# A fused attention, routing and channel-mixing kernel: the distance tables on VectorE and GpSimd, and the early gather some turns later

## The chip, the cores and the metric

One core of a Trainium2 chip runs the whole program. The metric is the device time of one execution in microseconds (us), as the median of three. The engines are named as in the profile: PE (TensorE, with PEld for its weight loads), DVE (VectorE), ACT (ScalarE), POOL (GpSimd) and SP (SyncE, here the issuer of most DMA transfers).

## The reference

Three stages follow one another, for 2 sequences of 768 tokens.

```
attention: 8 heads of 64, keys 0..7 for everybody and the last 96 keys
    scores = q k^T / 8 - slope[h] * dist;  masked;  a = softmax;  out = a v
mixture of experts: logits = x w_gate (8 experts), gate = sigmoid(x w_local)
    e = argmax(logits) where gate < 0.5 (or first token), else the token before's e
    out = softmax(logits)[e] * relu(x w1[e]) w2[e]
mixer: u = x + real(fft over sequence and channels);  out = u + relu(norm(u) w_ch1) w_ch2
```

`dist` is the distance from query to key (96 for a far global key), and `slope[h]` is 2 to the power of -(h+1) for 8 heads. A bias table for each head is therefore one distance table times one number.

## The kernel before, in words

**Attention.** A tile is 128 queries. The queries are worked in 24 units, numbered 0 to 23: tile i (0 to 5), sequence b (0 or 1), head group g (4 heads). Unit n stands for (i, b, g) in that order. A tile sees its own keys (the right third of a table, columns 256 to 383) and those of the tile before (columns 0 to 255, the far part with the left neighbour and the own keys side by side). Tile 0 has only the near part, so units 0 to 3 read only that.

The loop over n issues parts of four units in a written order. In round n it issues: `out(n-2, 1)` (ACT, PSUM to SBUF copy of turned probabilities), `keep(n-3)` (DVE, L180, the product with v out of the PSUM tile `sm`), `scores(n)` (PE), `rowmin(n)` (DVE, L142: four operations that add a head's bias and find the minimum), `step(k)`, `transp(n-1, 0)` (PE), `expo(n)` (ACT, L151: four exponentials) with `den` (POOL, L152), `out(n-1, 0)` (ACT), `step(k+1)`, `transp(n-1, 1)`, `upright(n-3)` (PE, L185), `norm(n-3)` (DVE), `step(k+2)`, `values(n-2)` (PE, L175), `step(k+3)`. Each engine works through its own instructions in the order of issue.

**Background work.** Each `step` takes one step of every generator in a list; I call it a turn. There are four to a unit. The generators are `tables` (bias tables), `far`, `Route.run` for a finished tile, and `ring.take`, which splits a piece of expert weights into a rounded half `hi` (ACT cast, L1006) and a remainder `lo` (a subtraction, L1008), in four parts of 128x512 with a cast and a subtraction in alternating turns. Four pieces are taken, from the turns in `TAKES`: from the third turns of units 12, 16, 20 and 22 on.

**Routing.** `Route.run(i)` gets logits from a tile (`lg`), finds the expert by `max` and `max_index`, transposes two flags into `rp` on PE (L516, L517, into the same PSUM tile `sm` that `keep` reads), scans along the tokens, finds the place of each token, and writes the rows to `xs` (SP) and the places to `list` (POOL, an indirect DMA, L568). The operations on X stand on POOL, and on DVE for the last tile. The route of tile i begins when unit 4i+3 is done, three units after its scores, so that of tile 4 starts in unit 22 and its `rp` comes right after `values(21)`.

After tile 2 the route also reads the first 128 entries of the list of expert 0 (`ent0`, SP, L579), `EARLY_READ` turns after the list was written, and `EARLY_GATHER` turns later gathers those rows into `x0` (POOL, L582). `early` computes expert 0 for them; its PE transposes of `x0` (L840) stand ahead of `values(23)` in PE's order. After the last unit, the route of tile 5, its list, `entries`, and `gathers` for the other experts follow one another; PE's next stage begins with the transposes of gathered rows (L1103).

**Bias tables.** All are ACT operations before (L222): four near tables before the loop, one more near table in each of the first four turns, eight far tables from unit 1 on.

Of the kernel before, what the change touches and what calls it, by code (L numbers as in the profile page):

```python
# [17 lines left out]
AF = mybir.ActivationFunctionType  # L18
ALU = mybir.AluOpType
# [5 lines left out]
B, H, S, D = 2, 8, 768, 64  # L25
E, F = 8, 1024
DM = H * D
NT = S // P
# [24 lines left out]
def load_kq(nc, st, io, i, pairs=((0, B * H // 2),)):  # L53

    if i >= NT:
        return
    for h, n in pairs:
        nc.sync.dma_start(st.kq[i][:, :, h:h + n], io["kq"][i, :, :, h:h + n])


def fast_attention(tc, st, io, route):
    nc = tc.nc
    V, A, G, T = nc.vector, nc.scalar, nc.gpsimd, nc.tensor
    KS = 3
    HP = B * H // 2
    with ExitStack() as ctx:
# [12 lines left out]
        four, last = views(st.raws, PIECES), views(more, NT - PIECES)  # L79
# [8 lines left out]
        def load_v(i):  # L88
            nc.sync.dma_start(vs[:, i % KS], io["v"][i])
# [118 lines left out]
        bias = res.tile([P, H, 384], F32, name="bias")  # L208
# [3 lines left out]
        dist, gl = room[:, :384], room[:, 512:512 + P]  # L212

        def local(r, c):
            d = dist[:, c:c + P]
            V.tensor_scalar(d, r, nl, -BIG, op0=ALU.is_ge, op1=ALU.mult)
            V.scalar_tensor_tensor(d, r, -1.0, d, op0=ALU.mult, op1=ALU.min)
            return d

        def tables(lo, hi):  # L220
            for h in range(H):
                A.activation(bias[:, h, lo:hi], dist[:, lo:hi], AF.Copy, scale=8.0 * 2.0 ** -(h + 1))  # L222
                yield

        def far():
            d = local(prev, 0)
            V.tensor_tensor(d, d, gl, op=ALU.max)
            load_v(1)
            yield
            yield from tables(0, 256)  # L230
            load_kq(nc, st, io, 2)
            load_kq(nc, st, io, 3)

# [3 lines left out]
        V.tensor_scalar(gl, glob, ng, -BIG, op0=ALU.is_ge, op1=ALU.mult)  # L237
        V.tensor_scalar(gl, gl, neg_nl, None, op0=ALU.min)
        V.tensor_tensor(dist[:, 256:], d, gl, op=ALU.max)
        near = tables(256, 384)  # L240
        for _ in range(4):
            next(near)
        bg = Background()
        bg.add(near)
# [13 lines left out]
        def step(k):  # L258

            for at, g, lo, hi in TAKES:  # L260
                if k == at:
                    bg.add(st.ring.take("e", g, cols=512, follow=False, part=(lo / 4, hi / 4), eng=lambda: G))
            route.slot = k % 4
            bg.step()
            for _ in range(AHEAD.get(k, 0)):
                next(ahead, None)

        for n in range(N + 3):
            if ok(n):
                i, b, g = units[n]  # L270
# [8 lines left out]
            if n == 1:  # L279
                bg.add(far())  # L280
# [10 lines left out]
            if ok(n - 3) and not ok(n - 1):  # L291
                upright(n - 3)
                norm(n - 3)
            step(k)
            if n < len(BUSY):
                keep_busy(nc, st, ps_t.tile([P, 2, 2, P], F32, name="tp").rearrange("p a b n -> p (a b n)"), BUSY[n])
# [4 lines left out]
            if ok(n - 1):  # L301
                out(n - 1, 0)
            step(k + 1)
            if ok(n - 1):
                transp(n - 1, 1)
                if ok(n - 3):
                    upright(n - 3)
                    norm(n - 3)
            step(k + 2)
            if ok(n - 2):  # L310
                values(n - 2)
# [17 lines left out]
def general_attention(tc, st, io, route):  # L329
# [3 lines left out]
    with ExitStack() as ctx:  # L333
# [18 lines left out]
        for i in range(NT):  # L352
# [11 lines left out]
            for b in range(B):  # L364
                x = rt.tile([P, ROW], F32, name="xrow")
                xs.append(x)
                for h in range(H):
# [16 lines left out]
                    V.tensor_tensor(t, t, far, op=ALU.add)  # L384
                    V.tensor_reduce(out=m, in_=t, op=ALU.max, axis=AX.X)
                    V.tensor_scalar(m, m, -1.0, None, op0=ALU.mult)
                    A.activation(t, t, AF.Exp, bias=m)
                    V.tensor_reduce(out=m, in_=t, op=ALU.add, axis=AX.X)
                    V.tensor_scalar(m, m, 1e-9, None, op0=ALU.add)
# [40 lines left out]
class Route:  # L430
# [31 lines left out]
    def run(self, i, xs, parts=None):  # L462
        nc, st, sb = self.tc.nc, self.st, self.sb
        V, A, G, T = nc.vector, nc.scalar, nc.gpsimd, nc.tensor
# [8 lines left out]
        pp = sm[:, 0:B]  # L473
        other = sm[:16, 4:5]
        last, first = i == NT - 1, i == NT - 4
        X = V if last else G
        to = lambda s, n=1: self.at(None if last else s, n)
        from2, from1 = st.pairs[:16, 0:16], st.pairs[:16, 16:32]
        lg = sb.tile([P, B, NL], F32, name="lg")
        if parts is not None:  # L480
            V.tensor_reduce(out=lg.unsqueeze(3), in_=parts.rearrange("p b h e -> p b e h"), op=ALU.add, axis=AX.X)
        else:
# [22 lines left out]
        for b in range(B):  # L505
            V.max(m8[:, b], l8[:, b])
        X.tensor_scalar(gn, z.to_broadcast([P, B, E]), GATE, None, op0=ALU.is_ge)
        for b in range(B):
            V.max_index(ix[:, b], m8[:, b], l8[:, b])
        yield from to(1)  # L510
        V.tensor_copy(fr, ix[:, :, :1])
        X.tensor_tensor(pe, l8, m8[:, :, :1].to_broadcast([P, B, E]), op=ALU.subtract)
        V.scalar_tensor_tensor(gf, z.to_broadcast([P, B, E]), GATE, fr.to_broadcast([P, B, E]),
                               op0=ALU.is_lt, op1=ALU.mult)
# [7 lines left out]
        yield from to(1)  # L522
        V.tensor_reduce(out=su, in_=pe, op=ALU.add, axis=AX.X)
        if last:
# [3 lines left out]
        if last:  # L528
# [3 lines left out]
                             op0=ALU.mult, op1=ALU.add)  # L532
# [8 lines left out]
                             op0=ALU.mult, op1=ALU.add)  # L541
# [23 lines left out]
        for b in range(B):  # L565
# [3 lines left out]
                out=st.list, out_offset=bass.IndirectOffsetOnAxis(ap=pos[:, b:b + 1], axis=0),  # L569
# [3 lines left out]
        if first:  # L573

            V.tensor_scalar(su[:1, 0], less, 0.0, None, op0=ALU.max)
            V.tensor_tensor(cu[:1, P - 1:], cu[:1, P - 1:], su[:1, 0], op=ALU.add)
            for _ in range(EARLY_READ):
                yield
            nc.sync.dma_start(st.ent0, st.list[1:P + 1])  # L579
            for _ in range(EARLY_GATHER):  # L580
                yield
            G.indirect_dma_start(  # L582
                out=st.x0, out_offset=None, in_=st.xs[:(i + 1) * B * P], in_offset=bass.IndirectOffsetOnAxis(ap=st.ent0[:, 0:1], axis=0),
# [43 lines left out]
DC = 258  # L627
TABLES = 4 * E
EARLY = 4
EARLY_READ = 5  # L630
EARLY_GATHER = 5
LATE = 4
TAKES = ((-46, 0, 0, 4), (-30, 1, 0, 4), (-14, 2, 0, 4), (-6, 3, 0, 4))
SPLIT = 6
# [710 lines left out]
class Mixer:  # L1345
# [46 lines left out]
    def tables(self):  # L1392
        v = lambda t, o, a, n: t[:, o:o + a * n].rearrange("p (a n) -> p a n", a=a)
        ring = self.st.ring
        (ch, cl), (sh, sl) = ring.get("t", 0), ring.get("t", 1)
        self.c1, self.s1 = ([v(t, 0, 3, SC) for t in x] for x in ((ch, cl), (sh, sl)))
        self.odd = self.s1[0][:1, 0]
        self.c2, self.s2 = ([v(t, 3 * SC, 2, DC) for t in x] for x in ((ch, cl), (sh, sl)))
# [389 lines left out]
@with_exitstack  # L1788
def program(ctx, tc, io):
    nc = tc.nc  # L1790
    ctx.enter_context(tc.manual_schedule())
    st = setup(tc, ctx, io)
    load_kq(nc, st, io, 0, ((0, 2), (2, 2), (4, 4)))
    with tc.tile_pool(name="ps_busy", bufs=1, space=PSUM) as ps:
        keep_busy(nc, st, ps.tile([P, 512], F32, name="busy"), 12)
    fast = nc.values_load(st.fast[0:1, 0:1], min_val=0, max_val=1)
    with tc.If(fast > 0) as arm:
        fast_attention(tc, st, io, Route(tc, st, io))
    with arm.Else():
        general_attention(tc, st, io, Route(tc, st, io))  # L1800
    post(tc, ctx, st)
    moe = Moe(tc, st, io)
    mix = Mixer(tc, st, io, moe)
    with ExitStack() as c2:
        moe.open(c2)
        moe.run()
        moe.close_x.close()
        mix.begin(ctx, ExitStack())
        moe.finish()
    with ExitStack() as c2:  # L1810
        mix.open(c2)
        mix.run(c2)
# [11 lines left out]
```

## Time and profile before

| what | value |
|---|---|
| median of 3 runs | 656.48 us (655.08 to 660.21) |
| profiled execution, its own time | 658.99 us |
| its span, first to last instruction | 657.2 us |
| mean granted PE clock | 0.976 |
| PE, DVE, ACT, POOL busy | 95%, 59%, 42%, 16% of the span |

The attention stage takes about the first 115 us of the span and the experts follow. The PE share counts pipelined matmuls and says little of how full PE is. What matters here are the places in which PE waits, what ends those waits, and the clock after them.

### The profile page before, as it was taken

How to read it: one execution, taken by the hardware profiler on the slowest of the kernel's cores; microseconds unless marked ns; L12 is line 12 of the kernel's file. 1: busy time of each engine (PE TensorE's matmuls, PEld its weight loads, DVE VectorE, ACT ScalarE, POOL GpSimd, SP SyncE). 2: the span in 40 equal slices, each digit the busy share in tenths (PEclk: the TensorE clock that was granted, in tenths of full speed). 3: DMA queues.
4: the chain of work that ended last, by engine and by line, in shares of the span. 5: the costliest groups of instructions: out<-in, count | busy, mean ns of one | idle time of the engine just before them, and what ended most of it. 6: DMA issues, size and time to landing. Idle time of an engine off the chain costs nothing.

```text
span 657.2 us, 9964 instructions
## 1 busy us (share of the span) xinstructions
PE 623.8 (95%) x3621; PEld 511.4 (78%) x3622; DVE 387.4 (59%) x891; ACT 278.9 (42%) x562; POOL 102.1 (16%) x147
## 2 busy tenths in 40 slices
PE   7999986869999999999999899999999999999997
PEld 3787865558998998897867787877788888888885
DVE  4687784429967888853369977899441131254112
ACT  5789891117654756563434533441221221141110
POOL 1126636330431333220100000000000000000000
PEclk9999995969999999999999899999999999999999
DMA  8354463258899798873062143443010010100001
GB/s 298 142 179 155 134 91 115 45 209 276 296 369 325 239 320 316 301 285 143 21 243 93 65 135 122 163 157 129 0 65 0 1 65 1 65 0 1 0 1 64
DMA packets 25187, 92.45 MB, mean 141 GB/s; under 512 B 7644, under 2 KB 8796, under 8 KB 17184
## 3 DMA queue, kind: packets, MB, share of 16 engines
q1 hardware_dynamic: 19376, 77.41, 34.6%
q0 software_dynamic: 4736, 10.56, 4.4%
q10 hardware_dynamic: 1008, 3.65, 1.5%
q8 instruction: 35, 0.57, 0.4%
q14 instruction: 32, 0.26, 0.2%
HBM read 81.00 MB, written 14.84 MB: 146 GB/s over the span
## 4 chain that ended last, share of the span: by engine, by line
PE 43%; DVE 7%; ACT 2%; issue 1%; DVEq 0%; ACTq 0%
PE h L1636 17%; PE acc L1652 5%; PE acc L1650 5%; PE acc L1651 5%; DVE dec L1032 1%; DVE dec L1034 1%; PE acc L1471 1%; PE y L1141 1%; PE acc L1457 1%; PE more L1191 1%; PE f L1602 1%; PE more L1141 1%; PE h L1191 1%; DVE dec L1030 1%; DVE dec L1028 1%
## 5 line engine op out<-in xcount | busy, mean ns | idle before, releaser
L1641 DVE SCALAR_TENSOR_TENSOR hl<-h,hh 128x512 fp32r<-128x512 f32 x48 | 33.1, 689 | 118.4 <-ACT hh L1640 118.4
L1640 ACT ACTIVATE hh<-h 128x512 fp32r<-128x512 f32 x48 | 28.7, 597 | 153.4 <-PE h L1636 153.3
L1008 DVE TENSOR_TENSOR wide<-raws,wide 128x1024 fp32r<-128x1024 f32 (+1 forms) x38 | 45.0, 1200 | 24.4 <-ACT wide L1006 24.1
L151 ACT ACTIVATE t<-t,nm 128x256 f32<-128x256 f32 (+1 forms) x96 | 45.8, 478 | 7.5 <-DVE nm L142 7.5
L1006 ACT CAST wide<-raws 128x1024 fp32r<-128x1024 f32 (+2 forms) x46 | 43.3, 957 | 5.6 <-PE acc L1652 3.4
L1636 PE MATMUL h<-un0h,wide 128*128 128x512 f32 (+1 forms) x136 | 42.5, 378 | 0.0
L1651 PE MATMUL acc<-wide,hh 128*128 128x512 f32 x96 | 37.7, 393 | 0.0
L142 DVE CUSTOM_DVE_ANT_0 t<-sp,bias 128x256 f32<-128x256 f32 (+1 forms) x96 | 32.7, 396 | 8.4 <-PE sp L133 3.9
L1650 PE MATMUL acc<-wide,hh 128*128 128x512 f32 x96 | 37.7, 392 | 0.0
L1652 PE MATMUL acc<-wide,hl 128*128 128x512 f32 x96 | 37.5, 391 | 0.0
L1164 ACT ACTIVATE hh<-h 128x512 fp32r<-128x512 f32 x28 | 16.7, 598 | 30.1 <-PE h L1161 23.1
L1071 POOL DMA_INDIRECT xg<-xs,ent x23 | 26.9, 1167 | 14.3 <-issue 6.1
L1161 PE MATMUL h<-xh,wide 128*128 128x256 f32 x192 | 28.4, 284 | 0.5 <-DVE hl L1165 0.4
L1636 PEld LDWEIGHTS h<-un0h,wide 128*128 128x128 f32 x136 | 25.0, 188 | 4.7
L161 PE MATMUL tp<-consts,t 128*128 128x128 f32 x176 | 27.0, 292 | 0.4
L1161 PEld LDWEIGHTS h<-xh,wide 128*128 128x128 f32 x192 | 25.5, 192 | 1.3 <-DVE hl L1165 0.6
L161 PEld LDWEIGHTS tp<-consts,t 128*128 128x128 f32 x176 | 20.0, 146 | 8.3 <-ACT p L167 3.0
L175 PE MATMUL sm<-p,vs 128*64 128x128 f32 x352 | 26.3, 293 | 0.0
L1636 PE MATMUL h<-un0l,wide 128*128 128x512 f32 (+1 forms) x68 | 25.7, 378 | 0.0
L1165 DVE SCALAR_TENSOR_TENSOR hl<-h,hh 128x512 fp32r<-128x512 f32 x28 | 19.2, 686 | 10.6 <-ACT hh L1164 6.7
L167 ACT COPY p<-tp 128x512 f32<-128x512 f32 (+1 forms) x48 | 24.2, 534 | 0.0
L175 PEld LDWEIGHTS sm<-p,vs 128*64 128x64 f32 x352 | 20.2, 145 | 4.1 <-issue 3.8
(454 smaller groups left out, 1658.2 us busy)
## 6 DMA issues: line engine op xcount, KB each, us to landing
raws<-we SPq DMA_DIRECT2D x30, 1024.0 KB
raws<-wm SPq DMA_DIRECT2D x17, 1024.0 KB
raws<-wmf SPq DMA_DIRECT2D x7, 1024.0 KB
wmf<-dec POOLq DMA_DIRECT2D x8, 512.0 KB
xs<-xrow SPq DMA_DIRECT2D x12, 260.0 KB
vs<-v SPq DMA_DIRECT2D x6, 512.0 KB
raws<-kq SPq DMA_DIRECT2D x3, 1024.0 KB
u<-x SPq DMA_DIRECT2D x6, 512.0 KB
```

The source lines that it names most:

```text
L142: V.tensor_tensor_reduce(out=u.t[:, x, :u.W], in0=u.sp[:, j, k, :u.W], in1=bias[:, 4 * u.g + x, u.b0:u.b0 + u.W], scale=-0.125, scalar=3.0 ...
L151: A.activation(u.t[:, x, :u.W], u.t[:, x, :u.W], AF.Exp, bias=u.nm[:, x:x + 1], scale=-1.0, accum_out=u.den[:, x])
L161: T.transpose(u.tp[k][:, j, c], u.t[:, 2 * k + j, c * P:(c + 1) * P], st.ident)
L175: T.matmul(turned[j * D:j * D + D, k], vs[:, ti % KS, u.h + 2 * k + j], u.p[:, 2 * k + j, c], start=c == 0, stop=c == len(tiles) - 1)
L1006: (first or nc.scalar.copy)(hi[:, cs], raw[:, cs])
L1008: (eng() if callable(eng) else eng or nc.vector).tensor_tensor(lo[:, cs], raw[:, cs], hi[:, cs].bitcast(F32), op=ALU.subtract)
L1161: T.matmul(ps[:, u], w[:, f], x[:, k], start=n == 0, stop=n == 11)
L1636: nc.tensor.matmul(ps[:, c], a[:, k], x[:, k, c], start=n == 0, stop=n == 11)
L1641: nc.vector.scalar_tensor_tensor(hl, ps, 0.0, hh.bitcast(F32), op0=ALU.max, op1=ALU.subtract)
L1650: T.matmul(acc[c], hh[:, cs], h2, start=first, stop=False)
L1651: T.matmul(acc[c], hh[:, cs], l2, start=False, stop=False)
L1652: T.matmul(acc[c], hl[:, cs], h2, start=False, stop=last)
```

## The change

The far tables are DVE multiplications. The near tables are four on ACT and four on POOL, all issued before the loop. A piece's subtractions get their engine from a new expression. X is DVE for the tiles 4 and 5 (before, for 5 alone). The read of `ent0` waits for 10 turns and the gather for 7 more (before 5 and 5).

```diff
-        def tables(lo, hi):
+        def tables(lo, hi, by):
             for h in range(H):
-                A.activation(bias[:, h, lo:hi], dist[:, lo:hi], AF.Copy, scale=8.0 * 2.0 ** -(h + 1))
+                out, slope = bias[:, h, lo:hi], 8.0 * 2.0 ** -(h + 1)
+                if by[h] is A:
+                    A.activation(out, dist[:, lo:hi], AF.Copy, scale=slope)
+                else:
+                    by[h].tensor_scalar(out, dist[:, lo:hi], slope, None, op0=ALU.mult)
                 yield
...
-            yield from tables(0, 256)
+            yield from tables(0, 256, [V] * H)
...
-        near = tables(256, 384)
-        for _ in range(4):
+        near = tables(256, 384, [A] * 4 + [G] * 4)
+        for _ in range(H):
             next(near)
...
-                    bg.add(st.ring.take("e", g, cols=512, follow=False, part=(lo / 4, hi / 4), eng=lambda: G))
+                    bg.add(st.ring.take("e", g, cols=512, follow=False, part=(lo / 4, hi / 4), eng=lambda: G if at < TAKES[-1][0] else V))
...
-        X = V if last else G
+        X = G if i < NT - 2 else V
...
-EARLY_READ = 5
-EARLY_GATHER = 5
+EARLY_READ = 10
+EARLY_GATHER = 7
```

## Rows read from the trace of the kernel before

**Rows 1.** Timeline of PE, 95 to 113 us: start, duration, instruction, [idle before, releaser].

```profile
95.92 1.09 PE L175 MATMUL sm<-p,vs 128*64 128x128 f32 x16
103.51 0.27 PE L516 MATMUL sm<-identb,gn 128*16 128x128 bf16 x1 [6.50 <-POOL gn L507]
...
111.12 1.06 PE L840 MATMUL tp<-consts,x 128*128 128x128 f32 x4
```

**Rows 2.** Timeline of POOL in the same stretch.

```profile
94.70 1.13 POOL L582 DMA_INDIRECT x<-xs,ent  x1 [5.05 <-ACT wide L1006]
...
103.15 0.31 POOL L507 TENSOR_SCALAR gn<-lg 128x16 bf16<-128x16 f32 x1
```

**Rows 3.** Waits of the SP queue, 70 to 100 us: total, times, longest; then SP's timeline.

```profile
SPq L579 <- DMA list<-dest,pos: 6.4, 1, 6.4
89.27 0.33 SPq L579 DMA_DIRECT2D ent<-list  x1
```

**Rows 4.** Busy time by stretch: PE, PEld, DVE, ACT, POOL, granted clock, DMA.

```profile
97.00:103.00 6.00, 0.01 (x2) 0.00 (x0) 3.10 (x6) 1.74 (x5) 5.37 (x8) 0.70 0.31 118
103.00:108.00 5.00, 4.49 (x26) 3.99 (x28) 1.82 (x5) 2.05 (x5) 4.74 (x8) 0.50 0.01 0
```

**Rows 5.** Timeline of PE in the first 21 us.

```profile
13.43 1.24 PE L50 MATMUL tp<-busy 128*128 128x512 bf16 x4 [1.41 <-ACT p L167]
14.73 1.11 PE L161 MATMUL tp<-consts,t 128*128 128x128 f32 x4
15.78 1.12 PE L175 MATMUL sm<-p,vs 128*64 128x128 f32 x8
...
18.88 0.66 PE L161 MATMUL tp<-consts,t 128*128 128x128 f32 x4
...
19.97 0.66 PE L175 MATMUL sm<-p,vs 128*64 128x128 f32 x8
```

**Rows 6.** Timeline of ACT in the first 21 us, table rows.

```profile
8.34 1.11 ACT L222 ACTIVATE bias<-vs 128x128 f32<-128x128 f32 x5 [4.66 <-DVE vs L239]
...
10.89 0.69 ACT L222 ACTIVATE bias<-vs 128x128 f32<-128x128 f32 x3
```

**Rows 7.** Groups by line and form, all of the span: busy us, mean ns | idle before.

```profile
L1028 DVE TENSOR_SCALAR dec<-dec 128x1024 f32<-128x1024 f32 x18 | 12.4, 688 | 0.6 <-ACT dec L1019 0.6
L455 POOL COPY iw<-consts 128x512 f32<-128x512 f32 x1 | 0.9, 917 | 0.0
L152 POOL TENSOR_SCALAR den<-den 128x4 f32<-128x4 f32 x24 | 5.5, 228 | 47.7 <-ACT t L151 47.3
L1424 DVE TENSOR_TENSOR fs<-u 128x512 f32<-128x512 f32 x6 | 4.1, 677 | 1.7 <-DMA u<-x 1.7
L1008 POOL TENSOR_TENSOR sl0l<-raws,sl0h 128x512 fp32r<-128x512 f32 x4 | 5.1, 1276 | 0.7 <-ACT sl0h L1006 0.4 <-issue 0.2
```

**Rows 8.** Timeline of DVE, from the first attention units and the last ones.

```profile
16.97 0.42 DVE L180 COPY o<-sm 128x256 f32<-128x256 f32 x1 [3.34 <-PE sm L175]
...
95.70 3.27 DVE L511 CAST fr<-ix 128x2 f32<-128x2 uint32 x1
...
114.15 0.41 DVE L180 COPY o<-sm 128x256 f32<-128x256 f32 x1
```

**Rows 9.** Timeline of ACT, 53 to 60 us: one unit while a weight piece is taken.

```profile
55.22 0.51 ACT L151 ACTIVATE t<-t,nm 128x256 f32<-128x256 f32 x1
...
57.20 0.57 ACT L167 COPY p<-tp 128x512 f32<-128x512 f32 x1
57.66 0.62 ACT L1006 CAST sl0h<-raws 128x512 fp32r<-128x512 f32 x1
...
59.18 0.52 ACT L151 ACTIVATE t<-t,nm 128x256 f32<-128x256 f32 x1
```

**Rows 10.** Timeline of PE: the flags of the route of tile 2, and the next stage.

```profile
66.58 0.22 PE L516 MATMUL sm<-identb,gn 128*16 128x128 bf16 x1 [0.74 <-DVE o L180]
...
137.89 1.94 PE L1103 MATMUL xtp<-consts,xg 128*128 128x128 f32 x8 [2.47 <-issue]
```

## The prediction

> **What bounds the kernel now.** I read PE's timeline around the end of the attention stage first, because all later stages wait for that end. After `values(21)` [rows 1] PE stands still for 6.50 us, until POOL has made the flags `gn` of tile 4. POOL is late because it waited 5.05 us for the early gather's entries [rows 2]. The row blames an ACT cast, but that cast was long done: SP waited 6.4 us for the list's writes to land and issued the read of `ent0` only at 89.27 [rows 3], and it landed about when the gather starts, at 94.70. Behind the gather POOL had subtractions of 1.28 us [rows 7], the rows of tile 3, and two indirect DMAs to do before `gn` at 103.15. Then I read the clock: in 97 to 103 us the granted clock is 0.70 on average, in 103 to 108 us it is 0.50, so 1.2 of 2.4 GHz, and it fell while PE was idle [rows 4]. So the wait is paid twice, once as a wait and once in slow matmuls behind it.
>
> The second place is the start. PE waits 1.41 us at 13.43 for a copy on ACT [rows 5], and behind it four transposes take 1.11 us and eight products 1.12, where the same work a unit later takes 0.66 and 0.66 [rows 5]. ACT is busy with tables there [rows 6]. In the middle of the stage, PE has two short waits, at the flags of tiles 2 and 3 (the row is the first of the two, 0.74 us) [rows 10].
>
> After the last `keep`, at 114.15 [rows 8], the route of tile 5, its list, the read and the gather follow each other up to 137.89 [rows 10], 23.7 us that no part of the change touches. What the end of the attention stage gains, the program gains.
>
> **The change part by part.** *Which engine subtracts.* The new expression compares `at` when it is called, not when it is made. The generator asks for its engine in later turns, when the loop over `TAKES` has run to its end and `at` is -6. The comparison -6 < -6 is false, so all 16 subtractions go to DVE, not only the last piece's four.
>
> *Start.* The second exponentials of ACT lose three tables ahead of them (0.69 us for three), and the first ones lose one of five (1.11 for five, about 0.2 each) [rows 6]: the copy on which PE waits comes 0.8 us earlier. From 13.43 on PE is the later one, so this 0.8 stays. If the clock does not fall then, transposes and products get back 0.45 + 0.46 [rows 5] as well, 0.9. The eight far tables leave ACT, but ACT was not what PE waited on there. On DVE, one costs between 0.17 (a quarter of 0.69 for 128x1024) and 0.69 [rows 7]; eight are 1.4 to 5.5 us. I take 0.3 each, 2.4 us, by the size of a 128x256 operation, and they lie in the 3.34 us in which DVE sat idle before 16.97 [rows 8]; without that cover the excess over 3.3 us would delay `rowmin(3)`. The four near tables on POOL cost between 0.23 (128x4) and 0.92 (128x512) each [rows 7], 0.4 by interpolation, so they end at about 10, when `rowmin(1)` wants the last at 10.2. At 0.92 they end at 12 and take back 0.5. Start: a gain of 0.3 to 1.7, I take 1.3, the middle of 0.8 and 1.7, since the clock can go either way.
>
> *The pieces of units 12 to 18.* A subtraction of this size is 0.68 us on DVE, 0.60 from start to start [rows 7]. The one in a fourth turn stands behind `norm` and ahead of `keep` and `rowmin` of the next unit, and its cast on ACT stands behind a whole set of exponentials. So a new circle arises: exponentials 1.98 us, copy 0.46, cast 0.62 [rows 9], subtraction 0.60, `keep` 0.34, first `rowmin` 0.45 with its way to ACT, together 4.45 us, against 3.96 us per unit now [rows 9]. There are two such turns in a piece: exponentials 0.9 to 1.3 us late, PE some 0.8 late. The short wait at the flags that follows [rows 10] takes most of that in. I take 0.3 for each of the first two pieces, bounds -0.3 and 1.4; below nothing, because POOL, freed of 1.28 us per subtraction, can make the flags sooner. Sum: -0.6.
>
> *The end.* I follow the same circle from unit 20, with pieces 2 and 3 back to back. The exponentials of unit 21 come 0.5 later than in the trace, of unit 22 1.0, of unit 23 1.5 (96.7). `values(21)` ends at 98.1 instead of 97.0. The flags of tile 4 are now DVE's and early enough; but they go into the PSUM tile that `keep(21)` reads, and PE waits for that `keep` at such flags already [rows 10]. It stands behind the subtraction of a fourth turn: exponentials end 98.7, copy 99.2, cast 99.7, subtraction 100.35, `keep` 100.7. So PE goes on at 100.8, after a wait of 2.7 us in place of 6.5. From there on at the full clock: transposes 1.0, `upright` 0.6, `values(22)` 1.0, `keep(22)` behind the last subtraction 104.3, `upright` 105.0, transposes of `x0` 105.5, `values(23)` 106.5, `rk` and, now on DVE, the rows of tile 4 (0.35 us) 107.1, `keep(23)` at 107.15: 7.0 earlier than 114.15. If the clock falls in the 2.7 us, as it did after PE went idle [rows 4], every PE step doubles, `keep(23)` comes at 111.5, and 2.65 remain. I take the middle, 4.8, since the clock came back at some point in all stretches.
>
> In this sum DVE's cast of 128x2 has at most 0.2 us, not 3.27 [rows 8]. In the trace that cast stuck while POOL's gather and subtraction ran. The Trainium skill (SBUF — State Buffer, "Who interferes with whom") says that DVE and GpSimd share a port pair as a lock for a whole instruction, and that casts and `tensor_scalar` of DVE can be caught by it. By that rule the row's 3.1 us vanish, as POOL has no subtractions left; if they stayed, the gain at the end would be about 3 us smaller. The same rule would speak against far tables on DVE beside near ones on POOL, but by the times above POOL is done first.
>
> *The gather.* SP reaches the read of `ent0` five turns later, but it waits for the same landing of the list, so it issues at 89.3 as before [rows 3]; what is queued behind it on SP (a patch of v) goes on as before. The gather now stands behind the indirect DMAs of tile 3 on POOL, issued about 95 to 97.4, so it finds its entries there and starts at 97.5. Behind it on POOL is only `den(23)`. The rows of `x0` are wanted at 105.
>
> *Sum.* 1.3 - 0.6 + 4.8 = 5.5 us. The profiled execution has 658.99 us (span 657.2 and 1.8 around it), so it would come to 653.5. It lies 2.5 above the median, from which I subtract the same: 656.48 - 5.5 = 651.0.
>
> **The rivals.** *The clock stays up.* For it: both waits that stood ahead of a fall get shorter, from 1.41 to about 0.6 and from 6.50 to 2.7. Against it: a wait of 1.41 us was enough for a fall [rows 5]. Then 1.7 - 0.3 + 7.0 = 8.4, a time of 648.1.
>
> *DVE is the bound.* Each piece is paid in full (0.7 twice), and the clock is low up to the end: 0.8 - 1.4 + 2.65 = 2.0, a time of 654.4. For it: a unit with two subtractions holds some 4.2 us of DVE work, against 3.96 of ACT.
>
> *`x0` comes too late*, the case on the slower side. Its transposes stand ahead of `values(23)` on PE, so all that follows waits. It decides from a landing at 105 on, and eats the 5.5 us at 110.5, 13 us after the gather's start. The list took over 6.4 us to land [rows 3], so a stretch to twice that is needed. With a landing 6.5 us after the want, a wait as long as the one removed, the time is 657.5; over 1% slower it gets from 12 us on.
>
> *The subtractions of the first three pieces stay on POOL*, if I read the expression wrongly. Then the two middle terms vanish and the end is about a microsecond better: gain 7.0, time 649.5.
>
> **How the numbers follow.** Chances: forecast 0.54, clock up 0.20, DVE bound 0.17, `x0` late 0.05, POOL keeps its part 0.04. A measurement of this kernel can tell about 1% (6.6 us). The forecast's own range is 648.5 to 653.5. For 8 in 10 I go from 647.5 (a little below the high clock's 648.1) to 655.5 (beyond the DVE case). Over 1% faster is below 649.9: the clock case, the POOL case and a quarter of the forecast, 0.37. Over 1% slower is only the late `x0`, 0.04 with its shorter waits taken out and some room for what I have not seen. Within 1%: 0.59.
>
> **What would show it.** No wait for POOL's `gn` ahead of L516 at 97 us, but one for DVE's `keep` of 2 to 3 us. All 16 subtractions L1008 of 128x512 on DVE at 0.68, none on POOL. `expo` waits for `rowmin` in the units with pieces. PE's wait at 13.43 shrinks to about 0.6. The early gather has no wait before it. If PE's wait at L516 is still above 4 us, or one appears before the transposes of `x0`, the sum is wrong at the end; if the clock is full from 97 us on, the gain is near 8.

## The result and the profile after

| | before | after |
|---|---|---|
| median, us | 657.17 (654.48 to 660.35, 20 runs) | 651.43 (648.52 to 654.37, 20 runs) |
| ratio to before | | 0.9912, 95% interval 0.9896 to 0.9929 |
| profiled execution, us (its span) | 658.99 (657.2) | 653.29 (651.5) |
| mean granted clock of it | 0.976 | 0.984 |

Forecast: 651.0. In the changed file the lines from 224 on stand four further down: the subtraction is L1012, its cast L1010, the flags L520 and L521, the gather L586, the list L572, the transposes of `x0` L844, the next stage's first transposes L1107.

PE's timeline of the changed kernel, from the start, the flags of tile 2, the end of the attention stage and the next stage:

```profile
12.61 1.02 PE L50 MATMUL tp<-busy 128*128 128x512 bf16 x4 [0.81 <-ACT p L167]
13.47 0.66 PE L161 MATMUL tp<-consts,t 128*128 128x128 f32 x4
14.06 0.66 PE L175 MATMUL sm<-p,vs 128*64 128x128 f32 x8
...
17.85 1.13 PE L133 MATMUL sp<-raws 64*128 64x256 f32 x8
...
64.00 0.22 PE L520 MATMUL sm<-identb,gn 128*16 128x128 bf16 x1
...
95.20 1.09 PE L175 MATMUL sm<-p,vs 128*64 128x128 f32 x16
99.00 0.22 PE L520 MATMUL sm<-identb,gn 128*16 128x128 bf16 x1 [2.70 <-DVE o L180]
...
99.20 1.91 PE L161 MATMUL tp<-consts,t 128*128 128x128 f32 x8
...
104.58 0.60 PE L844 MATMUL tp<-consts,x 128*128 128x128 f32 x4
...
110.27 0.27 PE L520 MATMUL sm<-identb,gn 128*16 128x128 bf16 x1 [1.95 <-DVE pos L568]
...
111.16 0.63 PE L858 MATMUL sp<-sl1h,wide 128*128 128x512 f32 x1
...
132.99 1.94 PE L1107 MATMUL xtp<-consts,xg 128*128 128x128 f32 x8 [3.23 <-issue]
```

Against [rows 1, 5, 10]: the first wait is 0.81 us instead of 1.41, and the transposes and products behind it take 0.66 each instead of 1.11 and 1.12. The wait of 0.74 at the flags of tile 2 is gone (64.00 for 66.58). At the flags of tile 4 the 6.50 us for POOL's `gn` have become 2.70 us for DVE's `keep`. The transposes of `x0` wait for nothing. The next stage starts 4.90 us earlier.

POOL and DVE, their timelines (against [rows 2, 8]), and SP's wait (against [rows 3]):

```profile
8.32 2.28 POOL L226 TENSOR_SCALAR bias<-vs 128x128 f32<-128x128 f32 x4 [1.08 <-DVE vs L243]
...
93.39 1.05 POOL L572 DMA_INDIRECT list<-dest,pos  x1 [0.71 <-DVE ix L513]
...
96.02 1.05 POOL L586 DMA_INDIRECT x<-xs,ent  x1 [0.31 <-issue]
```

```profile
95.74 0.16 DVE L515 CAST fr<-ix 128x2 f32<-128x2 uint32 x1
...
97.92 0.69 DVE L1012 TENSOR_TENSOR wide<-raws,wide 128x512 fp32r<-128x512 f32 x1 [0.45 <-ACT wide L1010]
98.53 0.42 DVE L180 COPY o<-sm 128x256 f32<-128x256 f32 x1
...
106.96 0.41 DVE L180 COPY o<-sm 128x256 f32<-128x256 f32 x1
```

```profile
SPq L583 <- DMA list<-dest,pos: 6.5, 1, 6.5
```

The gather no longer waits; the read of its entries waits for the list as before. PE's 2.70 us end with the `keep` at 98.53, which stands behind the subtraction at 97.92, which itself waited 0.45 us for its cast on ACT. The last `keep` stands at 106.96 for 114.15.

Groups by line and form (busy us, mean ns, idle before), against [rows 7]; and ACT's timeline at the tables and in two units with a piece, against [rows 6, 9]:

```profile
L1012 DVE TENSOR_TENSOR wide<-raws,wide 128x512 fp32r<-128x512 f32 x8 | 5.5, 684 | 0.6 <-ACT wide L1010 0.5
L1012 DVE TENSOR_TENSOR sl1l<-raws,sl1h 128x512 fp32r<-128x512 f32 x4 | 2.7, 682 | 0.2 <-ACT sl1h L1010 0.2
L1012 DVE TENSOR_TENSOR sl0l<-raws,sl0h 128x512 fp32r<-128x512 f32 x4 | 2.7, 681 | 0.2 <-ACT sl0h L1010 0.2
L226 DVE TENSOR_SCALAR bias<-vs 128x256 f32<-128x256 f32 x8 | 1.9, 288 | 0.0
...
L226 POOL TENSOR_SCALAR bias<-vs 128x128 f32<-128x128 f32 x4 | 2.1, 534 | 1.2 <-DVE vs L243 1.1
```

```profile
8.32 0.91 ACT L224 ACTIVATE bias<-vs 128x128 f32<-128x128 f32 x4 [4.64 <-DVE vs L243]
...
53.04 0.51 ACT L151 ACTIVATE t<-t,nm 128x256 f32<-128x256 f32 x1 [0.43 <-DVE nm L142]
...
57.54 0.51 ACT L151 ACTIVATE t<-t,nm 128x256 f32<-128x256 f32 x1 [0.43 <-DVE nm L142]
```

All 8 + 4 + 4 = 16 subtractions of 128x512 are on DVE. A far table costs 0.29 us there, a near one 0.53 on POOL. Two sets of exponentials start 4.50 us apart, each behind a wait for `rowmin`: this is the predicted circle.

Busy time by stretch (PE, PEld, DVE, ACT, POOL, granted clock, DMA), against [rows 4]:

```profile
97.00:103.00 6.00, 4.00 (x26) 3.60 (x27) 3.65 (x13) 3.52 (x8) 0.30 (x2) 0.72 0.55 46
103.00:108.00 5.00, 4.32 (x45) 3.21 (x39) 2.45 (x10) 0.59 (x1) 0.00 (x0) 1.00 0.05 17
108.00:112.00 4.00, 2.05 (x9) 1.44 (x8) 3.55 (x22) 0.47 (x2) 1.20 (x2) 0.69 1.03 335
112.00:118.00 6.00, 6.00 (x24) 4.08 (x23) 1.61 (x8) 0.00 (x0) 1.04 (x2) 0.63 0.28 106
```

The clock is low behind the wait of 2.70 us, back by 103, and low again behind the 1.95 us at the flags of tile 5, where the early expert's matmuls (L858) take 0.63 us each. That wait isn't new. The kernel before has the same one, and the matmuls behind it ran at the full clock there (PE's timeline of before):

```profile
117.46 0.22 PE L516 MATMUL sm<-identb,gn 128*16 128x128 bf16 x1 [1.95 <-DVE pos L564]
...
118.92 0.39 PE L854 MATMUL sp<-sl0h,wide 128*128 128x512 f32 x1
```

Over the 20 runs a mean clock of 0.992 goes with 648.5 to 649.8 us and one of 0.982 to 0.984 with 651.9 to 654.4.

**Where the time came from.** Lead over the profile before, at points of the path: 2.71 us at the scores of unit 4 (17.85), 2.58 at the flags of tile 2, 2.11 at those of tile 3 (80.44, before 82.55), 0.72 at the start of `values(21)`, 4.51 at the flags of tile 4, 7.19 at the last `keep`, 4.90 at the next stage, 5.7 at the end. So the path gained 2.7 at the start, lost 2.0 over the units with pieces, gained 6.5 at the end of the stage, lost 2.3 behind it, and 0.8 came in all later stages together, which is less than the single traces below differ by in those stages (2.7).

### The profile page after: what moved, and what is told of

Its sections match the earlier page's. It is cut to its first block, busy times and chain, and to the rows that moved or that the text cites. A ratio compares the mean times of both kernels' runs of the same rounds, so it can differ in the third digit from the quotient of the medians.

```text
span 651.5 us, 9965 instructions
## 1 busy us (share of the span) xinstructions
PE 622.5 (96%) x3621; PEld 509.7 (78%) x3622; DVE 394.2 (61%) x920; ACT 276.2 (42%) x550; POOL 83.5 (13%) x130
## 4 chain that ended last, share of the span: by engine, by line
PE 39%; DVE 11%; ACT 2%; issue 1%; DMA 1%; DVEq 0%; ACTq 0%
PE h L1640 17%; PE acc L1656 6%; PE acc L1655 6%; PE acc L1654 5%; DVE dec L1036 1%; DVE dec L1038 1%; PE y L1145 1%; PE more L1195 1%; PE more L1145 1%; PE h L1195 1%; DVE dec L1034 1%; DVE dec L1032 1%; DMA u<-x 1%; PE f L1606 1%; DVE wide L990 1%
## 5 line engine op out<-in xcount | busy, mean ns | idle before, releaser
L1012 DVE TENSOR_TENSOR wide<-raws,wide 128x1024 fp32r<-128x1024 f32 (+2 forms) x46 | 50.5, 1110 | 24.7 <-ACT wide L1010 24.5
L1010 ACT CAST wide<-raws 128x1024 fp32r<-128x1024 f32 (+2 forms) x46 | 43.3, 958 | 5.7 <-PE acc L1656 3.4
L175 PE MATMUL sm<-p,vs 128*64 128x128 f32 x352 | 24.8, 282 | 0.0
L1038 DVE SCALAR_TENSOR_TENSOR dec<-raws,dec 128x1024 int32<-128x1024 int32 x18 | 22.1, 1225 | 0.6
```

Source lines behind the costliest of these rows:

```text
L1010: (first or nc.scalar.copy)(hi[:, cs], raw[:, cs])
L1012: (eng() if callable(eng) else eng or nc.vector).tensor_tensor(lo[:, cs], raw[:, cs], hi[:, cs].bitcast(F32), op=ALU.subtract)
```

## The experiments

Each ran beside the kernel before on the same chip (medians of before 658.12 for the first four, 658.95 for the next four, 658.27 and 657.55 for the rest). Last `keep`, next stage and span are those of the one profiled execution, in us.

| label | ratio to before, interval | last keep | next stage | span |
|---|---|---|---|---|
| before | 1 | 114.15 | 137.89 | 657.2 |
| after | 0.9912, 0.9896 to 0.9929 | 106.96 | 132.99 | 651.5 |
| e1_tables | 0.9948, 0.9924 to 0.9973 | 112.58 | 138.53 | 657.6 |
| e2_no_tables | 0.9947, 0.9924 to 0.9970 | 108.60 | 132.11 | 650.5 |
| e3_text_engine | 0.9860, 0.9821 to 0.9899 | 104.48 | 129.62 | 647.8 |
| e4_sub_later | 0.9863, 0.9832 to 0.9894 | 106.63 | 131.79 | 650.6 |
| e5_turns | 0.9897, 0.9868 to 0.9925 | 107.90 | 132.81 | 651.1 |
| e6_no_turns | 0.9927, 0.9904 to 0.9950 | 107.87 | 131.80 | 649.4 |
| e7_x_pool | 0.9876, 0.9839 to 0.9913 | 104.30 | 129.02 | 647.4 |
| e8_late | 0.9900, 0.9871 to 0.9930 | 105.45 | 131.85 | 650.4 |
| e9_busy | 0.9886, 0.9861 to 0.9912 | 105.83 | 129.64 | 649.9 |
| e10_ahead | 0.9873, 0.9843 to 0.9903 | 105.14 | 128.35 | 646.9 |
| e11_gather6 | 0.9864, 0.9833 to 0.9895 | 103.32 | 126.75 | 645.6 |
| e12_both | 0.9833, 0.9801 to 0.9865 | 101.19 | 125.01 | 644.4 |

Span less next stage lies between 517.6 and 520.3 us in all fourteen: to within 2.7 us, what the edits change lies before the next stage. A caution: e3 and e10 are the same program up to the flags of tile 4, and e7 is up to the route of tile 4. They reach those flags at 96.59, 98.52 and 96.60; e10's execution waited 0.62 and 0.51 us at the flags of tiles 2 and 3 and the others not at all. So a difference under 2 us between two single traces proves nothing; a wait and its releaser do.

**The tables alone, and all but the tables.** Before with the new `tables` (e1), and the changed kernel with the old ones (e2). The lines of the change that tell the two apart, with the new body of `tables` left out:

```diff
-            yield from tables(0, 256)
+            yield from tables(0, 256, [V] * H)
...
-        near = tables(256, 384)
-        for _ in range(4):
+        near = tables(256, 384, [A] * 4 + [G] * 4)
+        for _ in range(H):
```

> The kernel before, with the new placing of the bias tables alone. In the changed kernel the scores of unit 4 start 2.71 us earlier (17.85 for 20.56), at the full clock. Theory (parts add up): the start is the tables' alone, and all behind it moves along, POOL's wait for the early gather too, so about 2.7 us remain in the end: ratio near 0.996. Rival (a fixed landing eats it): the list's writes and the entries of the early gather land when the transfers ahead of them allow, so POOL's wait grows by what the start gained and the ratio is 1.000.

> The changed kernel with the tables as before (ACT, four ahead of the loop). Theory: the subtractions, X and the turns alone give the rest, 3 us: ratio near 0.995; PE's wait at 13.4 us is 1.4 us again. Rival (the tables give nothing in the end): the ratio stays near 0.991.

Measured 655.38 and 655.07 us. 0.9948 times 0.9947 is 0.9895; the whole change has 0.9912: the parts add up, within their intervals. In e1 the wait for `gn` grew from 6.50 to 7.26 us, so a part of the early start is eaten as its rival has it, but 2.01 us of lead are left at those flags (101.50 for 103.51) and 1.57 at the last `keep`. Nothing of it is left at the next stage in e1's trace, the slowest of its ten runs, which had a granted clock of 0.79 in the 12 us after the last `keep` (before 1.00). PE's timeline of e2:

```profile
13.43 1.02 PE L50 MATMUL tp<-busy 128*128 128x512 bf16 x4 [1.42 <-ACT p L167]
14.51 0.66 PE L161 MATMUL tp<-consts,t 128*128 128x128 f32 x4
...
16.73 1.02 PE L50 MATMUL tp<-busy 128*128 128x512 bf16 x4 [0.33 <-ACT p L167]
...
19.49 1.13 PE L133 MATMUL sp<-raws 64*128 64x256 f32 x8
```

It has the old tables and the same first wait, 1.42 us, but the clock did not fall behind it (0.66 where [rows 5] have 1.11). So of the 2.71 us at unit 4, 20.56 - 19.49 = 1.07 are the clock of one execution, and 19.49 - 17.85 = 1.64 are the tables: 0.82 by the end of the first wait, the rest in a second one of 0.33 us and the work between.

**The first three pieces on POOL**, as the text of the line reads:

```diff
... (inside the call of ring.take)
-eng=lambda: G if at < TAKES[-1][0] else V
+eng=lambda at=at: G if at < TAKES[-1][0] else V
```

> The changed kernel with the engine fixed when a piece is added, so that the first three pieces are subtracted on POOL and only the last on DVE. Theory (the circle through DVE costs): units 12 to 22 have no subtraction ahead of a keep, exponentials are no longer late there, 1.5 to 2 us are won, the wait at the flags of tile 4 stays at 1.5 to 2.7 us for the last piece: ratio near 0.988. Rival (POOL's big operations hold up its list writes, flags and the gather, and DVE's small steps): the same as the changed kernel or worse, 0.991 to 0.995.

Measured 648.91 us, on the theory's side and a little beyond it. The trace shows no wait of PE between 50 and 92 us, and the flags of tile 4 come at 96.59 for 99.00, again behind 2.70 us for the same `keep`. Binding `at` late costs the changed kernel 2.5 us by the medians and 3.4 by the ratios (0.0052 of the time; the two come from different chips, and their intervals just touch).

**All subtractions on DVE, but every first and third of a piece a turn later**, behind the next unit's `rowmin` instead of ahead of its `keep` (`take` is called with `eng=V, skip=True`):

```diff
+            odd = skip and c // cols % 2 == 0
+            if odd:
+                yield
             (eng() ...).tensor_tensor(lo[:, cs], raw[:, cs], hi[:, cs]..., op=ALU.subtract)
-            yield
+            if not odd:
+                yield
```

> The changed kernel with every first and third subtraction of a piece one turn later, behind the next unit's rowmin instead of ahead of its keep; the same work on the same engines, casts as they were. Theory (the place of the subtraction makes the circle): exponentials no longer wait for rowmin in units with pieces, PE's wait at the flags of tile 4 falls from 2.70 us to under 0.8, and 2 to 5 us are won, the larger part where the clock then does not fall: ratio 0.984 to 0.988. Rival (DVE simply has too much work there, 4.2 us in a unit): the wait stays above 2 us and the ratio at 0.991.

Measured 649.83 us, the ratio of the theory. PE's timeline of it:

```profile
97.06 0.22 PE L520 MATMUL sm<-identb,gn 128*16 128x128 bf16 x1 [1.32 <-DVE o L180]
...
103.16 0.80 PE L844 MATMUL tp<-consts,x 128*128 128x128 f32 x4 [1.82 <-DMA x<-xs,ent]
```

The wait is halved, not under the 0.8 us expected; but it moves with the place of the subtraction (the `keep` starts at 96.60 for 98.53, while PE comes to the flags only 0.56 us earlier), so the subtraction ahead of `keep` is a cause of it. The other half of the theory failed: the exponentials still start 4.13 and 4.58 us apart with the first piece (52.56, 56.69, 61.27), the last behind a wait of 1.55 us for `rowmin`, and the flags of tiles 2 and 3 come at 63.95 and 79.99, hardly earlier than the 64.00 and 80.44 of the changed kernel. Now `x0` is late: the gather of the changed kernel has little to spare.

**Which part removed the 6.5 us.** e5 is e1 with the new turns alone; e6 is e3 with the old turns; e7 is e3 with the small work of tile 4 on POOL. The lines are against the changed kernel; e6 and e7 have the line of e3 besides:

```diff
 e5 and e7
-        X = G if i < NT - 2 else V
+        X = V if last else G
 e5, besides
-eng=lambda: G if at < TAKES[-1][0] else V
+eng=lambda: G
 e6
-EARLY_READ = 10
-EARLY_GATHER = 7
+EARLY_READ = 5
+EARLY_GATHER = 5
```

> Before with the new table placing and the new turns (read after 10, gather after 7), all sixteen subtractions on GpSimd and gn of tile 4 on GpSimd as before. Theory A, that the wait of 6.5 us at the flags of tile 4 was the gather holding GpSimd's queue: the wait falls under 3.5 us although GpSimd still has the subtractions and gn, and the ratio to before is 0.988 to 0.991 (0.995 from the tables alone, less some 3 us). Theory B, that GpSimd's subtractions hold gn back whatever the gather does: the wait stays above 5 us and the ratio is that of the tables alone, 0.994 to 0.996.

> The kernel with the first three pieces on GpSimd and the last on VectorE (0.986), with the gather back at its old turns (5 and 5). Theory A, that the gather's turn matters only through gn behind it on GpSimd, and gn is now on VectorE: the wait at the flags of tile 4 stays at 2.7 us and the ratio within 0.003 of 0.986. Theory B, that the turn is needed whatever engine has gn, since the gather's issue beside VectorE's two-input work holds VectorE (the cast of 3.3 us) or delays the lists: the wait is above 4 us and the ratio 0.989 to 0.993.

> The same kernel (0.986) with the late turns, but the small work of tile 4 (gn, pe, su and the row scale) on GpSimd as before. Theory A: with the gather behind gn and the lists done by 94.1 us, gn on GpSimd is ready before VectorE's keep of unit 21, the flags of tile 4 wait 2.7 us for that keep as with gn on VectorE, ratio 0.984 to 0.989: this part of the change is worth under 1 us. Theory B, that gn on VectorE is what removed the wait: the wait is above 4 us, released by GpSimd, ratio above 0.989.

Measured 652.15, 653.83 and 650.32 us: A, B and A. PE's timeline of e5:

```profile
95.54 0.22 PE L520 MATMUL sm<-identb,gn 128*16 128x128 bf16 x1 [1.35 <-POOL gn L511]
...
103.28 1.35 PE L185 MATMUL mi<-iw,o 128*128 128x148 f32 x4 [4.91 <-DVE o L180]
```

The turns alone take the wait at the flags from 7.26 us (e1's trace) to 1.35, with `gn` still on POOL. What is left of POOL's backlog, the last piece, shows one step later: 4.91 us for `keep` of unit 22, behind work of DVE that waits for POOL's `pe` and `su`. Putting the last piece on DVE is what removes that: e7 differs from e5 in that alone and waits 0.53 us there.

In e6 `gn` is early, on DVE, and still PE waits 5.44 us at the flags. DVE's and POOL's timelines of e6:

```profile
94.07 3.14 DVE L515 CAST fr<-ix 128x2 f32<-128x2 uint32 x1
```

```profile
92.94 1.13 POOL L586 DMA_INDIRECT x<-xs,ent  x1 [7.15 <-ACT wide L1010]
94.09 1.29 POOL L1012 TENSOR_TENSOR wide<-raws,wide 128x512 fp32r<-128x512 f32 x1
95.34 0.61 POOL L560 TENSOR_SCALAR xrow<-pe,su 128x8 f32<-128x8 f32 x2
95.92 1.26 POOL L1012 TENSOR_TENSOR wide<-raws,wide 128x512 fp32r<-128x512 f32 x1
97.26 0.25 POOL L152 TENSOR_SCALAR den<-den 128x4 f32<-128x4 f32 x1
```

The gather holds POOL until 94.07, its subtractions move behind it, and DVE's cast of 128x2, between the `rowmin` of unit 23 and the `keep` PE waits for, lasts 3.14 us: from the first of them to the end of the second. In the changed kernel, without any of POOL's subtractions, it has 0.16. The Trainium skill (SBUF — State Buffer, "Who interferes with whom") says that a DVE cast can contend with GpSimd for a shared port pair, which the first to issue holds for its whole instruction. The row agrees that the cast is held up, but for longer than one instruction: it outlasted several in a row. So the turn matters twice, by POOL's queue and by DVE, as long as POOL has subtractions; the changed kernel, where it has none, was not run with the old turns, so what the turn is worth there is not shown. The engine of tile 4's small work is worth less than the runs can tell: e7 waits the same 2.70 us as e3 (its row names POOL's `pe`, done at 96.60, with `keep` done at 96.55) and has 0.9876 for 0.9860.

**e3 with the last piece's first and third subtraction a turn later**, `skip=at == TAKES[-1][0]`:

> The same kernel (0.986) with the first and the third subtraction of the last piece, on VectorE, one turn later, behind the next rowmin. Theory: the wait at the flags of tile 4 falls from 2.70 to about 1.3 us, as it did in the kernel with all sixteen on VectorE; then x0 is late by 0.3 to 1.8 us (its gather issues at about 94.4 us and took 5.7 us to land there), so that 0 to 1.3 us are gained: ratio 0.983 to 0.987. Rival: the whole 1.4 us arrives, x0 is on time, ratio 0.982 to 0.984, and no wait at the transposes of x0.

Measured 652.44 us, worse than both expected. The gain at the flags is there and given back at `x0`; PE's timeline of e8:

```profile
96.08 0.26 PE L520 MATMUL sm<-identb,gn 128*16 128x128 bf16 x1 [0.52 <-DVE o L180]
...
102.96 0.63 PE L844 MATMUL tp<-consts,x 128*128 128x128 f32 x4 [2.09 <-DMA x<-xs,ent]
```

The gather, behind the lists of tile 3 on POOL, issued at 96.45 (94.35 in e3) and took 6.5 us to the transposes. By the last `keep` e8 is 0.97 us behind e3, and another 1.26 are lost up to the next stage, at a clock of 0.62 in the 12 us after that `keep` (0.86 in e3). So that order was tried as well, e8 with `EARLY_GATHER = 6`, which puts the gather ahead of those lists:

> The kernel with the last piece's subtractions one turn later (0.990), with the gather one turn earlier, which puts it ahead of the lists of tile 3 on GpSimd. Theory, that x0 arriving late (a wait of 2.09 us at its transposes) is all that kept that kernel from its gain: the gather issues as soon as the entries are there (some 6 us behind the issue of their read, so at about 94 us), x0 is there by 100.5 us, no wait at its transposes, ratio 0.982 to 0.986. Rival, that the gather, waiting there, holds the lists and VectorE as at the old turns: an instruction of VectorE takes over 1 us near 94 us, and the ratio is 0.988 or above.

Measured 648.47 us, ratio 0.9864, just above the upper end of the theory. PE's timeline of e11:

```profile
96.05 0.22 PE L520 MATMUL sm<-identb,gn 128*16 128x128 bf16 x1 [0.53 <-DVE o L180]
...
100.94 0.60 PE L844 MATMUL tp<-consts,x 128*128 128x128 f32 x4
```

The gather issued at 93.24, `x0` is on time, and no instruction of DVE from 91 to 98 us lasts over 0.7. The next stage comes 2.9 us before that of e3; in the medians this is not told apart from e3 (648.91).

**The clock.** The changed kernel with eight idle matmuls inside the wait of 2.70 us:

```diff
+            if n == N:
+                keep_busy(nc, st, ps_t.tile([P, 2, 2, P], F32, name="tp")..., 8)
             step(k)
```

> The changed kernel with eight more idle matmuls (128x512, nothing reads them) on TensorE between the values of unit 21 and the flags of tile 4, inside its wait of 2.70 us. Theory, that the low clock behind that wait is part of what the wait costs: the clock stays at full speed there, the eight transposes behind the flags take 1.1 us instead of 1.9, the four products 0.7 instead of 1.2 and the values 1.1 instead of 1.4, so that some 1.7 us are gained by 104 us, and the ratio is 0.986 to 0.990. Rival, that the clock falls in one of the next waits anyway and takes the same back there: full speed at 99 to 103 us but a ratio of 0.990 to 0.993, as the changed kernel's 0.991.

Measured 651.37 us. PE's timeline of e9:

```profile
97.51 1.89 PE L50 MATMUL tp<-busy 128*128 128x512 bf16 x8 [1.12 <-ACT p L167]
99.33 0.22 PE L522 MATMUL sm<-identb,gn 128*16 128x128 bf16 x1
...
99.54 1.09 PE L161 MATMUL tp<-consts,t 128*128 128x128 f32 x8
```

The clock stayed at 1.00 from there to 124 us, behind the wait of 1.95 us too, the eight transposes take 1.09 instead of 1.91, and the next stage comes 3.35 us earlier than in the changed kernel. Of these 3.35 us, 1.6 are left in the span, and the ratio, 0.9886, has an interval that overlaps both expectations. What the low clock costs in this stage is shown by the durations of the same instructions in the two traces; that the idle matmuls keep it up in other executions, or win time over many runs, is not.

**e3 with three early matmuls ahead of the flags of tile 5:**

```diff
-AHEAD = dict(enumerate([1, 1, 0, 3, 0, 0, 0, 0, 3, 3, ...
+AHEAD = dict(enumerate([1, 1, 0, 3, 0, 0, 0, 3, 0, 3, ...
```

> The kernel with the first three pieces on GpSimd (0.986), and three matmuls of the early expert one turn earlier, so that they stand ahead of the flags of tile 5 instead of behind them, inside that wait of 1.95 us. Theory, that the early expert's matmuls behind that wait, at low clock, are what gave back 2.3 us ahead of the next stage: the row counts of tile 5 come 1.2 us earlier or more, the next stage starts before 128.5 us (129.6), ratio 0.981 to 0.985. Rival, that the next stage waits for transfers that don't depend on these matmuls: ratio within 0.002 of 0.986.

Measured 649.92 us: by the ratio the rival, by the trace the theory (next stage 128.35). The wait at tile 5 is 1.08 for 1.95, but the clock was full in this execution, which alone does much. Not told apart.

**Both, e11 with those matmuls:**

> The kernel with the last subtractions later and the gather ahead of the lists (0.986), and the three early matmuls ahead of the flags of tile 5. Theory, that the two waits add: the wait at the flags of tile 4 is 0.5 us and that of tile 5 1.1 us, and the next stage starts at 125.5 to 126.5 us (126.8 without the move, which gave 1.0 to 1.3 us in the kernel where it was tried), ratio 0.983 to 0.986. Rival, that TensorE's clock in the later stages takes such gains back: next stage as early as that, ratio 0.986 to 0.990.

Measured 646.53 us, ratio 0.9833, at the theory's lower end and the lowest of all, though its interval overlaps those of e3 and e11. PE's timeline of e12:

```profile
94.70 0.22 PE L520 MATMUL sm<-identb,gn 128*16 128x128 bf16 x1 [1.44 <-DVE o L180]
...
104.52 0.22 PE L520 MATMUL sm<-identb,gn 128*16 128x128 bf16 x1 [1.08 <-DVE pos L568]
...
125.01 1.94 PE L1111 MATMUL xtp<-consts,xg 128*128 128x128 f32 x8 [3.74 <-issue]
```

The wait at tile 4 is 1.44 us and not 0.5, since PE got there earlier (`values(21)` at 92.17, in e11 94.43), and the next stage is half a microsecond ahead of the expected range. The six runs lie within 646.1 to 647.1.

## Why the prediction was right, point by point

The sum, 5.5 us, met a lead of 5.7 at the end of the profiled execution and of 5.7 in the medians. The mechanism at both ends of the stage was as predicted. That the number came so close is in part luck: terms were off in opposite directions, and two of the differences, 1.07 at the start and 2.3 behind the stage, go with the clock of single executions.

- *Which engine subtracts*: right, all 16 are on DVE, and e3 shows the other reading of the line. The price was too low: the forecast gave that rival 1.5 us over itself, the runs 2.5 to 3.4 (by medians and by ratios).
- *Start*, 1.3 us taken, 2.71 in the trace. The mechanism held (the copy 0.82 earlier, forecast 0.8). Two sizes were off. The tables gave 1.64 without the clock, since a second wait of 0.33 us and what lies between went too, where I counted only the first wait. And the half of 0.9 that I took for the clock was 1.07, which e2 shows to be the luck of one execution: a wait of 1.4 us was followed by the low clock in one trace and not in another. That "a wait of 1.41 us was enough for a fall" was too strong as a ground for the next execution.
- *Far and near tables*: 0.29 us on DVE, forecast 0.3; 0.53 on POOL, forecast 0.4. The last near one ended at 10.6, and one `rowmin` waited 0.31 us for it. PE shows nothing of it.
- *The pieces of units 12 to 18*, -0.6: 2.71 to 2.11, so 0.60; period 4.50, forecast 4.45. The circle is shown, the match of the 0.60 is luck. It counts on the waits of 0.74 and 0.61 us that before's trace has at the flags of tiles 2 and 3 to take in most of the delay. e1, with the new tables and the pieces on POOL, has neither wait and is at these flags at 63.19 and 78.65. Against it the pieces on DVE cost 0.81 and 0.98, 1.79 together; e3 says the same (1.88).
- *The end*: wait of 2.7 us for `keep(21)` forecast, 2.70 measured. From tile 3's flags to the last `keep` the lead grew by 7.19 - 2.11 = 5.08; I had taken 4.8 as a mean of two clock cases, and the clock was low for half of it (99 to 103 us). e4 and e8 show that most of this wait hangs on the place of the subtraction.
- *The cast*: 0.16 us, forecast at most 0.2. Its cause was put too widely, "POOL's gather and subtraction": e6 shows it lasting from one subtraction to the end of the next, with the gather's issue already over.
- *The gather*: no wait, start at 96.02 (97.5 forecast). `x0` was on time. In e4 and e8 PE came to these transposes 3.2 and 3.7 us earlier and waited 1.82 and 2.09 us for the rows: this rival decides as soon as the stage ends some 2 us earlier.
- *The 23.7 us "that no part of the change touches"*: this step failed. They became 132.99 - 106.96 = 26.03. PE idled the same 1.95 us at the flags of tile 5 in both traces, but then the granted clock was 0.63 to 0.69 from 108 to 118, and `rk` of tile 5 waited 3.01 us behind the early expert's slow matmuls, where it waited 0.91 before. Traces with the full clock in the 12 us after the last `keep` (before, e2, e6, e9, e10, e11, e12) have 23.2 to 23.9 us for the stretch; after, e1, e3, e4, e5, e7 and e8, with a mean of 0.62 to 0.86 there, have 24.7 to 26.4. "What the end of the attention stage gains, the program gains" holds only as far as the clock is the same. What decides the clock there stays open: with that same wait it was full in five traces and low in seven.

So the start gave 1.4 more, the end of the stage 0.3 more, and the stretch behind it took 2.3: a lead of 4.9 at the next stage, 0.6 less than the sum. The 0.8 us that made it 5.7 came later and was in no term.

## What to carry to other kernels

When an engine's queue is freed of one late item, look at what else that item pushed together: here the gather that waited for its entries moved POOL's subtractions beside another engine's small cast, and the moved turn with the new tables (e5, 0.9897) was worth as much as the whole change (0.9912). A lambda in a loop that a generator calls later reads the loop variable's last value; here that put three pieces on the busier engine and cost 2.5 to 3.4 of the 9.2 us that e3 gains. A stretch that an edit doesn't touch still changes with the clock that it meets; forecast it with two prices, and compare single traces by waits and releasers, not by a microsecond or two of position.

## What the runs showed of the hardware that was not expected

- Some small DVE instructions are held up beside POOL's two-input subtractions, one of them for a run of several: the cast of 128x2 took 3.27 us before, 3.14 in e6, and 0.16 without them. In e5 the scan of 16x128 took 1.13 us and the compare 1.30 while POOL subtracted, 0.47 and 0.25 in the changed kernel. Others kept their times beside the same subtractions: in e5 the reciprocal of 128x4 at 100.03 took 0.14 us and the product of 128x256 at 100.39 0.41.
- The same wait of 1.4 us in the same place was followed by matmuls at 1.11 in one execution and 0.66 in another, so a single trace doesn't tell what a wait costs in clock. The wait of 1.95 us at the flags of tile 5 shows it over more traces: matmuls of 0.39 us behind it before, 0.63 in the changed kernel.
- From the issue of the read of `ent0` to the issue of a gather that waits for it pass 5.4 to 6.7 us (89.27 to 94.70 before, 86.98 to 92.94 in e6, 86.54 to 93.24 in e11). From the gather's issue to transposes of `x0` that wait for it pass 6.5 to 6.7 (e8, e4). An earlier turn than these times allow gains nothing.
